# Squared-ReLU attention with a routed feed-forward on one core: order of the work at the end of a slot and of a chunk, and the share of squares on ScalarE

## The chip, the core and the metric

One core of a Trainium2 chip. TensorE (PE in the profile, PEld for its weight loads) multiplies, VectorE is DVE, ScalarE is ACT, GpSimd is POOL, SyncE (SP) issues nearly all transfers. The metric is device time in microseconds of one execution, lower is better; the kernel before has a median of 2253.57 us over 3 runs.

## What is computed

```python
scores = (1/S) * z @ z.T                    # z: (8, 3136, 64)
attn   = np.maximum(scores, 0.0) ** 2
x      = u * (attn @ v)                     # u, v: (8, 3136, 256), S = 3136
# then, for each batch: the 128 rows of x with the largest x @ w_gate go through
xe + sigmoid(score) * (np.maximum(xe @ w1, 0) @ w2)      # w1: (256, 1024), w2: (1024, 256)
```

All in float32. Since z @ z.T is symmetric, a square of one block serves, turned, as the square of the mirrored block.

## The kernel before

The eight batches follow one another. A batch has seven chunks of output columns, five of 512, one of 256 and one of 320 (`chunks_of`), and a chunk has thirteen slots: twelve take two 128-row blocks of the summed dimension each, the thirteenth the 64 rows left over. The text numbers chunks 0 to 6 and slots 0 to 12.

A slot that is new computes its scores (`scores`, L478): six matmuls into one pair of banks `sc` (L510), a ReLU into `a` (L514, ACT), then squares. The square is kept as two parts for the matmuls, `hi` (L524, ACT, rounded) and `lo`, the exact square less `hi` (L614, on POOL or DVE). So the exact square `a` is needed too: either on ACT (L530) or on DVE (L534), as the rule at L529 says from a running estimate of each engine's backlog (`busy`). New squares that a later chunk needs are turned on DVE (L577, L595, L557) and stored to DRAM; a slot that is old reads them back (`qk`) and makes `hi` by a copy (L474). Scores run three slots ahead (`LEAD`).

`mix` (L649) writes the PE work of one slot: twelve steps of two matmuls (L641), which use the upper and the lower 64 rows at once and add to four banks `acc`. A phase is the half of the steps that goes to one pair of these banks. An ordinary slot runs eight steps with `hi`, then `between` (the scores of the slot three ahead), then four with `lo`. Slot 0 runs phase 0, `between`, phase 1. Slot 11, the ending one, runs its phase 0 (`one`), then the phase 0 of slot 12 (the 64 rows, `Vr`), which closes two banks, then its phase 1 (`two`). The small matmuls of routing and feed-forward (`beside`) stand in front of step 4.

There are five `acc` banks in turn, so a new chunk has one free bank and takes the others from the old chunk: its phase 0 needs the first bank that ACT copied out (`finish_early`, L720, two copies into `x`), its phase 1 the other copied bank and the one that the first DVE instruction of `finish` releases (L732). `finish` (L724) adds the other two banks to `x` (L732), multiplies by u (L736), and after that turns and stores the result (L745, L752).

Instructions of an engine run in the order in which this program writes them. What follows a `mix` on DVE and ACT (the `posts` of the small matmuls and the squares, turns and `lo` of the slot three ahead) is written behind it.

Of the kernel before, what the change touches and what calls it, by code (L numbers as in the profile page):

```python
# [15 lines left out]
ALU = mybir.AluOpType  # L16
# [72 lines left out]
def attention_then_routed_ffn(ctx: ExitStack, tc: tile.TileContext, zt, ut, v, wg, w1, w2, cst, cst16, keys, outs, at, cap):  # L89
# [388 lines left out]
    def scores(k):  # L478
        b, c, js, is_old = slots[k]
        if is_old:  # L480
            return old_scores(k)
        n = len(js)
        w = CHUNKS[c][1]
        mov = Z[b, c]
        hi = work.tile([P, 2, CH], F32R, name="hi", tag="hi2", bufs=LEAD)
        a = work.tile([P, 2, CH], F32, name="a", tag="a", bufs=3)
        ps = ps_s.tile([P, 2, CH], F32, name="sc", tag="sc")
        if n == 1:
            w = w // 2
            o = js[0] * P - WIDE  # L490
            for i, (z, m) in enumerate(((ZHe, 0), (ZHe, 1), (ZLe, 0))):
                for q in range(2):
                    rows = slice(q * 64, q * 64 + 64)
                    nc.tensor.matmul(  # L494
                        ps[:, q, :w], z[rows, o : o + P], mov[m][rows, q * w : (q + 1) * w], start=i == 0, stop=i == 2
                    )
            a, hi = a[:, 0, :w], hi[:, :, within(c)]
            for q in range(2):
                rows = slice(q * 64, q * 64 + 64)
                nc.scalar.activation(a[rows], ps[rows, q, :w], AF.Relu)  # L500
            nc.scalar.activation(hi[:, 0, :w], a, AF.Square)
            spend(act=0.39 + 0.0024 * w)
            lows.append((k, a, hi[:, :, :w], (), lambda: nc.vector.tensor_tensor(a, a, a, op=ALU.mult)))
            return
        if is_second(k):
            mov, w = [x.rearrange("p (f x) -> p f x", x=P)[:, :, P // 2 :] for x in mov], w // 2
        for i, (high, m) in enumerate(((True, 0), (True, 1), (False, 0))):
            for q in range(2):
                rows = slice(q * 64, q * 64 + 64)
                nc.tensor.matmul(  # L510
                    ps[:, q, :w], stationary(high, js[0] // 2, q), mov[m][rows], start=i == 0, stop=i == 2
                )
        a = a[:, :, :w]
        nc.scalar.activation(a, ps[:, :, :w], AF.Relu)  # L514
        act = 0.13 + 0.0016 * w
        spend(act=act)
        if is_second(k):
            by = lambda x: x.rearrange("p q (f x) -> p q f x", x=P)
            pieces = [(lambda x: by(x)[..., 64:], a.rearrange("p q (f x) -> p q f x", x=64))]
            pieces.append((lambda x: by(x)[..., :64], fetched[b, c, c].rearrange("p f (q x) -> p q f x", q=2)))  # L520
        else:
            hi = hi[:, :, within(c)]
            pieces = [(lambda x: x, a)]
        nc.scalar.activation(pieces[0][0](hi), pieces[0][1], AF.Square)  # L524
        for view, src in pieces[1:]:
            nc.scalar.copy(view(hi), src)
        spend(act=act * len(pieces))
        dve = 0.15 + 0.00208 * w
        if busy["act"] + act < busy["dve"] + dve + (0.16 + 0.00236 * w if turns(k) else 0.0):  # L529
            nc.scalar.activation(a, a, AF.Square)  # L530
            spend(act=act)
            square = lambda: None
        else:
            square = lambda: nc.vector.tensor_tensor(a, a, a, op=ALU.mult)  # L534
            spend(dve=dve)
        lows.append((k, a, hi, pieces, square))

    def turns(k):
        b, c, js, _ = slots[k]
        return (c < WHOLE or c == WHOLE and b < B - 1) and js[0] * P >= sum(CHUNKS[c])  # L540
# [108 lines left out]
    def mix(k, beside, between):  # L649


        b, c, js, _ = slots[k]
        assert k in parts
        first, last = k % SLOTS == 0, js[0] == NJ
        ending = k % SLOTS == SLOTS - 2
        if first:
            banks = [ps_a.tile([P, CH], F32, name="acc", tag="acc")[:, : CHUNKS[c][1]] for _ in range(2 * NK)]
            acc[b, c] = [[banks[0], banks[2]], [banks[3], banks[1]]]
        if last:
            todo = steps_of(k, 1)  # L660
            turn = 3
        else:
            one, two = (steps_of(k, phase) for phase in range(2))
            if ending:
                todo, turn = [*one, *steps_of(k + 1, 0), lambda: finish_early(b, c), *two], 6
            elif first:
                todo, turn = [*one, *two], 6
            else:
                todo, turn = [*one[:4], *two[:4], *one[4:], *two[4:]], 8
        for n, step in enumerate(todo):  # L670
            if n == min(4, turn):
                for op in beside:
                    op()
            if n == turn:
                between()
            step()
        parts.pop(k)
        if turn == len(todo):
            if last:
                near.extend(finish(b, c))  # L680
            between()
# [42 lines left out]
    def finish(b, c):  # L724

        scored = c < NCH - merged(b)
        c0, w = CHUNKS[c]
        NB = w // Q
        xT = chunk.pop((b, c))
        whole, sums = early.pop((b, c))  # L730
        for h in reversed(range(NK)):
            nc.vector.scalar_tensor_tensor(  # L732
                sums[h], acc[b, c][1 - h][h], SCALE * SCALE, sums[h], op0=ALU.mult, op1=ALU.add
            )
        for h in range(NK):
            nc.vector.tensor_tensor(xT[:, h, :w], sums[h], xT[:, h, :w], op=ALU.mult)  # L736
        spend(dve=0.2 + 0.0046 * w)
        del acc[b, c]
        if c == 0:
            gate[b] = tail.tile([P, TP], F32, name="gate", tag="gate")  # L740
        x = whole[:, :NB]
        wx = xT.rearrange("p h c -> p (h c)").rearrange("p (f r) -> p f r", r=RUN)[:, :NB]

        def turn(h):
            nc.vector.transpose(x[:, :, h, :], xT[:, h, :w].rearrange("p (f q) -> p f q", q=Q))  # L745
            spend(dve=0.1 + 0.0013 * w)
            if h < NK - 1:
                return
            to = outs[b][c0 : c0 + w, :].rearrange("(f t) (g r) -> g t f r", t=Q, g=NG)
            runs = x.rearrange("p f h r -> p f (h r)")  # L750
            for g in range(NG):
                stores.append(lambda g=g: nc.sync.dma_start(to[g], runs[g * Q : (g + 1) * Q]))  # L752
            if scored:
                nc.gpsimd.tensor_tensor(  # L754
                    wx,
                    runs,
                    consts["wg_run"].rearrange("p (o r) -> p o r", o=1).broadcast_to([P, NB, RUN]),
                    op=ALU.mult,
                )
                spend(pool=0.1 + 0.0042 * w)  # L760

        def add():
            nc.vector.tensor_reduce(gate[b][:, c0 // Q : c0 // Q + NB], wx, axis=AX.X, op=ALU.add)
            spend(dve=0.1 + 0.0023 * w)

        def flip(i):

            h, i = i % NK, i // NK
            o, n = groups_of(w)[i]
            if h == 0:  # L770
                flipped.append(ps_a.tile([P, 512], F32, name="flip", tag="acc"))
            nc.tensor.transpose(flipped[i][:n, h * P : (h + 1) * P], xT[:, h, o : o + n], consts["ident"])

        def store(i):
            o, n = groups_of(w)[i]
            to = whole.rearrange("p f h r -> p (f h r)")[:n, i * D : (i + 1) * D]
            src = flipped[i][:n, :D].rearrange("p (h g r) -> p g h r", h=NK, g=NG)
            nc.scalar.copy(to.rearrange("p (g h r) -> p g h r", g=NG, h=NK), src)
            stores.append(lambda: nc.sync.dma_start(outs[b][c0 + o : c0 + o + n, :], to))

        flipped = []
        turns = [lambda h=h: turn(h) for h in range(NK)]
        if scored:
            return [([], turns), ([], [None, add])]
        spread, seen = scores_of(b, c, xT)
        if c == NCH - 1:
            flips = [([lambda i=i, h=h: flip(i * NK + h) for h in range(NK)], lambda i=i: store(i)) for i in range(-(-w // P))]
            return [(spread, None), ([], [lambda q=q: seen(q) for q in range(2)]), *flips]
        return [(spread, turns), ([], [lambda q=q: seen(q) for q in range(2)])]
# [949 lines left out]
```

## Time and profile before

| | before |
|---|---|
| runs | 2240.06, 2253.57, 2254.3 us (median 2253.57) |
| the profiled execution | 2252.5 us, span of its instructions 2250.7 us |
| mean granted TensorE clock | 0.978 of full speed |
| busy share PE / DVE / ACT / POOL | 92% / 79% / 60% / 64% |
| matmuls | 19700, of them 16800 of L641 |

Times within a row are microseconds, unless ns stands there. In rows of waits an arrow points to the engine and line that ended the wait. In rows of the timeline the first number is the start from the span's beginning, the second the time from the start of the first to the end of the last of the instructions that the row merges (xN), and brackets hold the idle time of the engine before it.

### The profile page before, as it was taken

The page shows a single profiled execution, that of the slowest core. Times are in us where ns is not written, and L with a number is a line of the kernel's source. Part 1 is how long each engine was busy: PE and PEld are TensorE (multiplying, and loading weights), DVE is VectorE, ACT ScalarE, POOL GpSimd, SP SyncE. Part 2 cuts the span into 40 slices and gives each one's busy share as a digit, 9 for nine tenths or more (in the row PEclk, how much of TensorE's full clock was granted, in tenths as well). Part 3 has the DMA queues.
Part 4 walks back from the last instruction along what each step waited for, and adds up shares of the span by engine and source line. Part 5 has one row for each costly group of instructions (what it writes and reads, how often), then busy time and mean ns, then how long its engine had stood idle before and what let it go on. Part 6 is the DMA issues. An engine that isn't in the chain of part 4 may idle for free.

```text
span 2250.7 us, 51225 instructions
## 1 busy us (share of the span) xinstructions
PE 2081.2 (92%) x19700; PEld 1743.9 (77%) x19700; DVE 1772.1 (79%) x2771; ACT 1360.9 (60%) x1846; POOL 1438.8 (64%) x773
## 2 busy tenths in 40 slices
PE   7899989999898999989999999999999999889897
PEld 5688978779776797778877788777887789667686
DVE  8887799757997589976889668986698887867665
ACT  6565667556774476745676556664576656666452
POOL 5776587646875467855678457765578665766452
PEclk9999999999999999999999999999999999999998
DMA  5678757785577865777567776667756687546841
GB/s 168 190 214 233 209 164 226 213 224 171 173 206 197 222 180 167 210 208 218 175 186 192 206 217 191 181 185 193 229 175 198 161 206 214 168 132 165 210 141 70
DMA packets 450869, 426.94 MB, mean 190 GB/s; under 512 B 136576, under 2 KB 377792, under 8 KB 447808
## 3 DMA queue, kind: packets, MB, share of 16 engines
q1 hardware_dynamic: 449488, 421.18, 66.0%
q8 instruction: 154, 2.52, 0.5%
q0 software_dynamic: 768, 2.10, 0.3%
q14 instruction: 91, 0.75, 0.1%
q10 hardware_dynamic: 368, 0.39, 0.1%
HBM read 248.94 MB, written 174.60 MB: 188 GB/s over the span
## 4 chain that ended last, share of the span: by engine, by line
PE 39%; DVE 23%; DMA 15%; issue 8%; SPq 6%; ACT 5%; POOL 3%; DVEq 0%; ACTq 0%; POOLq 0%
PE acc L641 33%; DVE aT L577 5%; DMA qk<-squares 5%; DVE a L534 4%; PE sc L510 3%; DMA squares<-aT 3%; DVE lo L614 3%; DVE ut L736 3%; POOL lo L614 2%; ACT hi L524 2%; DMA qk<-squares_narrow 1%; ACT a L514 1%; DMA squares_narrow<-aT 1%; SPq L752 1%; DMA zst<-in_zt 1%
## 5 line engine op out<-in xcount | busy, mean ns | idle before, releaser
L641 PE MATMUL acc<-hi,V 64*128 64x512 f32 (+2 forms) x10752 | 1320.5, 367 | 31.0 <-ACT x L720 20.5
L641 PEld LDWEIGHTS acc<-hi,V 64*128 64x128 f32 x10752 | 1008.7, 188 | 209.7 <-ACT x L720 39.7
L614 POOL TENSOR_TENSOR lo<-a,hi 128x1024 fp32r<-128x1024 f32 (+1 forms) x320 | 721.2, 2255 | 554.2 <-DVE a L534 336.1
L641 PE MATMUL acc<-lo,V 64*128 64x512 f32 (+2 forms) x5376 | 742.2, 369 | 57.0 <-POOL lo L614 43.7
L641 PEld LDWEIGHTS acc<-lo,V 64*128 64x128 f32 x5376 | 523.5, 188 | 145.7 <-POOL lo L614 67.6
L514 ACT ACTIVATE a<-sc 128x1024 f32<-128x1024 f32 (+2 forms) x345 | 327.5, 949 | 378.8 <-PE sc L510 329.8
L474 ACT CAST hi<-qk 128x1024 fp32r<-128x1024 f32 (+2 forms) x327 | 279.9, 858 | 257.6 <-PE acc L641 195.8
L534 DVE TENSOR_TENSOR a<-a 128x1024 f32<-128x1024 f32 (+1 forms) x203 | 288.6, 1422 | 146.5 <-ACT hi L524 144.6
L524 ACT ACTIVATE hi<-a 128x1024 fp32r<-128x1024 f32 (+2 forms) x345 | 339.7, 985 | 35.4 <-PE acc L641 8.7
L614 DVE TENSOR_TENSOR lo<-qk,hi 128x1024 fp32r<-128x1024 f32 (+2 forms) x213 | 299.4, 1417 | 77.9 <-ACT hi L474 70.4
L577 DVE STREAM_TRANSPOSE aT<-a 128x512 f32<-128x512 f32 (+1 forms) x494 | 317.2, 680 | 50.8 <-DMA squares<-aT 30.4
L614 POOL TENSOR_TENSOR lo<-qk,hi 128x1024 fp32r<-128x1024 f32 (+2 forms) x114 | 230.0, 2023 | 97.4 <-issue 51.3
L736 DVE TENSOR_TENSOR ut<-x,ut 128x512 f32<-128x512 f32 (+2 forms) x112 | 184.8, 1689 | 1.9
L754 POOL TENSOR_TENSOR ut<-x,w_run 128x1024 f32<-128x1024 f32 (+2 forms) x52 | 130.2, 2503 | 77.6 <-DVE x L745 69.2
L126 POOL TENSOR_TENSOR V<-vst,V 128x512 fp32r<-128x512 f32 x92 | 168.6, 1844 | 15.4 <-ACT V L125 13.3
L530 ACT ACTIVATE a<-a 128x1024 f32<-128x1024 f32 (+2 forms) x142 | 144.1, 1015 | 4.5
L510 PE MATMUL sc<-Z,ZH 64*128 64x512 f32 x480 | 107.5, 380 | 5.3 <-ACT a L514 5.2
L732 DVE SCALAR_TENSOR_TENSOR x<-acc,x 128x512 f32<-128x512 f32 (+2 forms) x112 | 64.4, 616 | 54.4 <-ACT x L720 48.8
L510 PE MATMUL sc<-Z,ZL 64*128 64x512 f32 x480 | 105.2, 371 | 0.0
L510 PE MATMUL sc<-Zl,ZH 64*128 64x512 f32 x480 | 104.7, 371 | 0.0
L500 ACT ACTIVATE a<-sc 64x256 f32<-64x256 f32 (+2 forms) x112 | 39.4, 351 | 91.8 <-PE sc L494 86.8
L126 POOL TENSOR_TENSOR ZL<-zst,ZH 64x256 fp32r<-64x256 f32 x70 | 69.6, 995 | 13.3 <-ACT ZH L125 10.7
(219 smaller groups left out, 1867.0 us busy)
## 6 DMA issues: line engine op xcount, KB each, us to landing
squares<-aT SPq DMA_DIRECT2D x160, 512.0 KB, 3.3
qk<-squares SPq DMA_DIRECT2D x320, 256.0 KB, 6.2
squares_narrow<-aT SPq DMA_DIRECT2D x320, 128.0 KB, 3.8
qk<-squares_narrow SPq DMA_DIRECT2D x80, 512.0 KB, 4.4
out<-x SPq DMA_DIRECT2D x162, 128.0 KB, 3.5
ut<-in_ut SPq DMA_DIRECT2D x40, 512.0 KB, 5.6
vst<-in_v SPq DMA_DIRECT2D x158, 128.0 KB, 3.4
zmv<-in_zt SPq DMA_DIRECT2D x78, 128.0 KB, 4.1
```

What stands on the lines that cost most here:

```text
L126: (lo_on or nc.vector.tensor_tensor)(lo, src, hi.bitcast(F32), op=ALU.subtract)
L474: nc.scalar.copy(by(hi), src)
L510: nc.tensor.matmul(ps[:, q, :w], stationary(high, js[0] // 2, q), mov[m][rows], start=i == 0, stop=i == 2)
L514: nc.scalar.activation(a, ps[:, :, :w], AF.Relu)
L524: nc.scalar.activation(pieces[0][0](hi), pieces[0][1], AF.Square)
L530: nc.scalar.activation(a, a, AF.Square)
L534: square = lambda: nc.vector.tensor_tensor(a, a, a, op=ALU.mult)
L577: nc.vector.transpose(to, a[:, q].rearrange("p (m t a) -> p m t a", m=GT, a=Q))
L614: on.tensor_tensor(view(lo), src, view(hi).bitcast(F32), op=ALU.subtract)
L641: nc.tensor.matmul(bank[g][h][:, cols[g]], V[b, j][rows, i, h], mov[rows], start=(b, c, g, h) not in opened, stop=len(js) == 1 and n == 2,)
L736: nc.vector.tensor_tensor(xT[:, h, :w], sums[h], xT[:, h, :w], op=ALU.mult)
L754: nc.gpsimd.tensor_tensor(wx, runs, consts["wg_run"].rearrange("p (o r) -> p o r", o=1).broadcast_to([P, NB, RUN]), op=ALU.mult,)
```

## The change

Four edits. The test at L529 lets a square go to ScalarE as long as its backlog is less than DVE's plus 1.0 and the cost on DVE (before: ScalarE's backlog with this square added had to be less than DVE's with its own cost). `mix` writes `beside` behind the last step of a slot, where it stood in front of step 4. In the ending slot `between` moves from behind `one` to behind the early steps of slot 12, and `finish_early` stands in front of it. `finish` adds within the PSUM bank (`rest`) and multiplies from there, bank by bank, where it added into `x` for both banks first.

```diff
@@ scores
-        if busy["act"] + act < busy["dve"] + dve + (0.16 + 0.00236 * w if turns(k) else 0.0):
+        if busy["act"] < busy["dve"] + 1.0 + dve + (0.16 + 0.00236 * w if turns(k) else 0.0):
             nc.scalar.activation(a, a, AF.Square)
@@ mix
             if ending:
-                todo, turn = [*one, *steps_of(k + 1, 0), lambda: finish_early(b, c), *two], 6
+                early_steps = steps_of(k + 1, 0)
+                todo, turn = [*one, *early_steps, *two], len(one) + len(early_steps)
...
         for n, step in enumerate(todo):
-            if n == min(4, turn):
-                for op in beside:
-                    op()
             if n == turn:
+                if ending:
+                    finish_early(b, c)
                 between()
             step()
+        for op in beside:
+            op()
@@ finish
         for h in reversed(range(NK)):
-            nc.vector.scalar_tensor_tensor(
-                sums[h], acc[b, c][1 - h][h], SCALE * SCALE, sums[h], op0=ALU.mult, op1=ALU.add
-            )
-        for h in range(NK):
-            nc.vector.tensor_tensor(xT[:, h, :w], sums[h], xT[:, h, :w], op=ALU.mult)
+            rest = acc[b, c][1 - h][h]
+            nc.vector.scalar_tensor_tensor(rest, rest, SCALE * SCALE, sums[h], op0=ALU.mult, op1=ALU.add)
+            nc.vector.tensor_tensor(xT[:, h, :w], rest, xT[:, h, :w], op=ALU.mult)
```

New line numbers: L722 is L720 of before, L735 is L732, L736 stays.

Over the program 119 of 203 squares of L534 leave DVE for ACT (L530: 142 before, 261 after). Since the backlog estimates shift, 55 of the `lo` subtractions also leave POOL for DVE.

First place, PE, slot 9 of chunk 2 (of batches 1 to 5): `ahead` is a routing count, two small matmuls that read `upto` of DVE. Before:

```order
L641 MATMUL acc<-hi,V 128x512 x8
L1038 LDWEIGHTS c_86
L1038 MATMUL ahead<-upto,c_86 98x2
L1039 LDWEIGHTS c_86
L1039 MATMUL ahead<-upto,c_86 98x2
L641 MATMUL acc<-hi,V 128x512 x8
L494 MATMUL sc<-Z,ZHe 128x256 x2
L494 MATMUL sc<-Zl,ZHe 128x256 x2
L494 MATMUL sc<-Z,ZLe 128x256 x2
L641 MATMUL acc<-lo,V 128x512 x8
```

Now:

```order
L641 MATMUL acc<-hi,V 128x512 x16
L494 MATMUL sc<-Z,ZHe 128x256 x2
L494 MATMUL sc<-Zl,ZHe 128x256 x2
L494 MATMUL sc<-Z,ZLe 128x256 x2
L641 MATMUL acc<-lo,V 128x512 x8
L1038 LDWEIGHTS c_86
L1038 MATMUL ahead<-upto,c_86 98x2
L1039 LDWEIGHTS c_86
L1039 MATMUL ahead<-upto,c_86 98x2
```

The pair moved past eight matmuls with `hi`, the scores and eight with `lo`, to the end of its slot.

Second place, the end of chunk 2. On ACT, before:

```order
L474 CAST hi<-qk 128x1024
L514 ACTIVATE a<-sc 128x1024
L524 ACTIVATE hi<-a 128x1024
L720 ACTIVATE x<-acc 128x512 x2
L474 CAST hi<-qk 128x1024
```

Now:

```order
L474 CAST hi<-qk 128x1024
L722 ACTIVATE x<-acc 128x512 x2
L514 ACTIVATE a<-sc 128x1024
L524 ACTIVATE hi<-a 128x1024
L474 CAST hi<-qk 128x1024
```

The two copies out of `acc` moved ahead of the ReLU and the square of the next chunk's slot 1. On DVE at the same place, before:

```order
L614 TENSOR_TENSOR lo<-qk,hi 128x1024
L534 TENSOR_TENSOR a<-a 128x1024
L732 SCALAR_TENSOR_TENSOR x<-acc,x 128x512 x2
L736 TENSOR_TENSOR ut<-x,ut 128x512 x2
L595 STREAM_TRANSPOSE aT<-a 128x8x32 x2
```

Now:

```order
L614 TENSOR_TENSOR lo<-qk,hi 128x1024
L534 TENSOR_TENSOR a<-a 128x1024
L735 SCALAR_TENSOR_TENSOR acc<-acc,x 128x512
L736 TENSOR_TENSOR ut<-acc,ut 128x512
L735 SCALAR_TENSOR_TENSOR acc<-acc,x 128x512
L736 TENSOR_TENSOR ut<-acc,ut 128x512
L595 STREAM_TRANSPOSE aT<-a 128x8x32 x2
```

Sum and product now alternate; the exact square of the next chunk's slot 1 still stands in front of them on DVE (at the ends of chunks 2 and 3 of every batch).

Third place, DVE at the end of chunk 0, where slots 0 and 1 of the next chunk are both new. Before:

```order
L557 STREAM_TRANSPOSE aT<-a 128x256
L534 TENSOR_TENSOR a<-a 128x1024
L595 STREAM_TRANSPOSE aT<-a 128x8x32 x2
L534 TENSOR_TENSOR a<-a 128x1024
L732 SCALAR_TENSOR_TENSOR x<-acc,x 128x512 x2
L736 TENSOR_TENSOR ut<-x,ut 128x512 x2
L951 TENSOR_SCALAR ge,own<-gates,k_sb 128x392
```

Now:

```order
L557 STREAM_TRANSPOSE aT<-a 128x256
L595 STREAM_TRANSPOSE aT<-a 128x8x32 x2
L614 TENSOR_TENSOR lo<-a,hi 128x1024
L735 SCALAR_TENSOR_TENSOR acc<-acc,x 128x512
L736 TENSOR_TENSOR ut<-acc,ut 128x512
L735 SCALAR_TENSOR_TENSOR acc<-acc,x 128x512
L736 TENSOR_TENSOR ut<-acc,ut 128x512
L951 TENSOR_SCALAR ge,own<-gates,k_sb 128x392
```

Both squares left for ACT, and the `lo` of the next chunk's slot 0, which was POOL's, stands on DVE behind the turns L595.

## Rows read from the trace of the kernel before

**Rows 1.** The page: span, and busy time and share of each engine.

```profile
span 2250.7 us, 51225 instructions
...
PE 2081.2 (92%) x19700; PEld 1743.9 (77%) x19700; DVE 1772.1 (79%) x2771; ACT 1360.9 (60%) x1846; POOL 1438.8 (64%) x773
```

**Rows 2.** Waits of PE: for whom, us in total, times, longest.

```profile
PE acc L641 <- POOL lo L614: 43.7, 44, 3.3
PE ahead L1038 <- DVE upto L1031: 20.5, 7, 3.7
PE acc L641 <- ACT x L720: 20.5, 32, 1.8
PE tot L903 <- DVE cnt L897: 15.6, 9, 4.8
...
PE h L1358 <- DVE xs L126: 8.6, 5, 2.8
...
PE gate L862 <- DVE gate L763: 6.5, 4, 1.8
```

**Rows 3.** Timeline, batch 3: chunk 2, slot 9, then an undisturbed slot of chunk 4.

```profile
958.97 0.16 PE L1038 MATMUL ahead<-upto,c 98*98 98x2 bf16 x1 [3.69 <-DVE upto L1031]
...
1048.63 1.98 PE L641 MATMUL acc<-hi,V 64*128 64x512 f32 x16
...
1050.44 0.28 PE L494 MATMUL sc<-Z,ZHe 64*128 64x256 f32 x2
...
1050.80 1.09 PE L641 MATMUL acc<-lo,V 64*128 64x512 f32 x8
```

**Rows 4.** Timeline, batch 4: end of chunk 2 and start of chunk 3.

```profile
1241.76 0.40 PE L510 MATMUL sc<-Z,ZH 64*128 64x512 f32 x2
...
1242.45 0.52 PE L641 MATMUL acc<-hi,Vr 64*128 64x256 f32 x6
...
1244.03 1.06 ACT L524 ACTIVATE hi<-a 128x1024 fp32r<-128x1024 f32 x1 [0.34 <-PE acc L641]
...
1244.99 1.06 ACT L720 ACTIVATE x<-acc 128x512 f32<-128x512 f32 x2
1245.12 1.23 DVE L534 TENSOR_TENSOR a<-a 128x1024 f32<-128x1024 f32 x1 [3.44 <-ACT hi L524]
...
1245.62 1.19 PE L641 MATMUL acc<-hi,V 64*128 64x512 f32 x7 [0.68 <-ACT x L720]
...
1246.26 1.28 DVE L732 SCALAR_TENSOR_TENSOR x<-acc,x 128x512 f32<-128x512 f32 x2
...
1247.58 4.62 DVE L736 TENSOR_TENSOR ut<-x,ut 128x512 f32<-128x512 f32 x2
1247.58 1.29 PE L641 MATMUL acc<-hi,V 64*128 64x512 f32 x8
```

**Rows 5.** Timeline, batch 3: start of chunk 1, DVE.

```profile
881.15 0.77 DVE L595 STREAM_TRANSPOSE aT<-a 128x256 f32<-128x256 f32 x2 [2.51 <-DMA squares_narrow<-aT]
```

**Rows 6.** Timeline, batch 3: chunk 0, slots 2 and 3, PE.

```profile
841.75 1.21 PE L641 MATMUL acc<-lo,V 64*128 64x512 f32 x8 [1.34 <-POOL lo L614]
...
847.41 0.88 PE L641 MATMUL acc<-lo,V 64*128 64x512 f32 x4 [1.93 <-DVE lo L614]
```

**Rows 7.** Groups of DVE by line and shape: busy us, mean ns, idle before.

```profile
L534 DVE TENSOR_TENSOR a<-a 128x1024 f32<-128x1024 f32 x156 | 246.7, 1582 | 141.1 <-ACT hi L524 139.6
...
L736 DVE TENSOR_TENSOR ut<-x,ut 128x512 f32<-128x512 f32 x80 | 152.8, 1948 | 1.4
...
L732 DVE SCALAR_TENSOR_TENSOR x<-acc,x 128x512 f32<-128x512 f32 x80 | 51.4, 684 | 40.7 <-ACT x L720 36.9 <-DMA vst<-in_v 3.8
...
L1393 DVE TENSOR_TENSOR hl<-hT,hh 128x512 fp32r<-128x512 f32 x16 | 10.8, 687 | 12.2 <-ACT hh L1389 12.2
```

**Rows 8.** Stretches of time, PE: length, busy (instructions), granted clock, DMA share, GB/s.

```profile
958.00:962.00 4.00, 3.03 (x24) 0.81 0.44 136
962.00:966.00 4.00, 4.00 (x30) 0.76 0.88 218
...
941.00:945.00 4.00, 4.00 (x39) 1.00 0.87 272
```

## The prediction

> **What bounds the kernel now.** I read the page first: PE is busy 92% of a span of 2250.7 us, DVE 79%, POOL 64%, ACT 60% [rows 1]. PE is the bound, so an edit is worth what it takes out of PE's idle time, about 170 us, and of the time at a lower clock. Next I read whom PE waits for [rows 2]. Three kinds matter here: for POOL's `lo` (43.7 us), for the copies out of `acc` at a chunk's start (20.5 us), and for DVE in front of a small matmul (`ahead`, `tot`, `h`, `gate`: 20.5 + 15.6 + 8.6 + 6.5 = 51.2 us). Then I read the timeline at these places [rows 3 to 6], the durations on DVE by shape [rows 7], and the granted clock behind a long wait [rows 8].
>
> **The change, part by part.**
>
> *Small matmuls at the slot's end.* In slot 9 of chunk 2 PE stands 3.69 us, with matmuls of the slot ready behind, until DVE has `upto` [rows 3]. Now eight matmuls with `hi`, the scores and eight with `lo` come first. Sixteen take 1050.44 - 1048.63 = 1.81 us, so eight take 0.9; scores of half width take 0.36 (1050.80 - 1050.44) [rows 3], of full width 0.69 (1242.45 - 1241.76) [rows 4]. I take eight `lo` at the same 0.9. The shift is thus 2.2 us, or 2.5. The seven `ahead` waits keep 20.5 - 7 x 2.2 = 5.1 us. Of nine `tot` waits the longest, 4.8, keeps 2.3; the others have a mean of 1.35 and vanish. Of `h` 0.3 stays, of `gate` nothing. 7.7 of 51.2 us stay: **-43.5 us**. Bounds: 0, if DVE's result comes later by as much, and -51.2. What waits now instead are the instructions on DVE and ACT that read these matmuls, 2 us later than before, with `lo` of the slot three ahead queued behind them; PE needs that two slots later (a slot without scores is 24 matmuls, 2.7 us), which covers it. Without the cover it would cost the same 2 us back.
>
> *Copies ahead of the squares.* At the start of chunk 3 PE idles 0.68 us for the first copy, which starts at 1244.99 because the square at 1244.03 stood in front of it [rows 4]. Now the copies start when the small group of slot 12 is done. That group takes about 0.36 us (as scores of that width), so its last matmul ends near 1242.3, the copies run to 1243.4, and PE finds its bank. What is late next is the second half of slot 0, which needs the first bank that DVE releases. The chain there: ReLU to 1244.5 (taken as long as the square), square to 1245.6, where it ended at 1245.09 before, exact square on DVE 1.23 us to 1246.8, sum 0.64, product 0.69, release at 1248.2. Before, the sum alone released it, at 1246.26 + 0.64 = 1246.9, and PE came at 1247.58. PE would now come at 1247.58 - 0.68 = 1246.9, waits 1.3 us and goes on 0.6 later than before. At the start of chunk 4 the order on DVE is the same and no scores (0.69) stand between PE's halves, so there it is 1.3 later. Eight batches: **+15 us**. Where DVE has neither exact square nor `lo` in front (starts of chunks 5 and 6) a part of the wait of 20.5 us is won: **-2 us**.
>
> *DVE in front of the sum at chunk 1.* The turns L595 sat until 881.15 for a transfer that read their buffer, and took 0.77 us [rows 5]. `lo`, which POOL did, now stands behind them on DVE: 881.9 + 1.2 = 883.1, at best. Phase 0 of slot 0 needs it about 0.9 us after the slot begins, near 881.4. That is up to 1.8 us of wait in place of 0.68 plus a lost pair of matmuls (0.23), or 0.9 worse at eight starts, +7; nothing if the buffer comes free earlier. **+4 us**.
>
> *Finish within the bank.* The product from SBUF and SBUF takes 1948 ns, the sum with one operand in PSUM 684, and L1393, a difference with one operand in PSUM and this shape, 687 [rows 7]. I take 684 for the new sum (its output in PSUM is not in the trace; bounds 0 saved, and 1948) and 687 for the product. 80 products of this shape save 1.26 us each, 101 us of DVE. DVE idles 21%, so I count this at nothing; its effect is in the next item.
>
> The Trainium skill (VectorE: DVE Perf Modes, Rules for kernel authors) speaks against this edit: it advises a copy from PSUM to SBUF first where many operations follow on a matmul's output. By the page's fixed costs, 120 against 58 cycles at 0.96 GHz, a PSUM operation is 65 ns dearer, an estimate of 15 us of DVE over 224 operations and 7 us on the path (two per chunk start), and the sum of this text would be 2203. The trace shows the opposite here, 687 against 1948 ns.
>
> *More squares on ScalarE, and chunk 0.* 119 squares leave DVE, at up to 1582 ns [rows 7], and cost ACT about 1.06 us each (as the square at 1244.03 [rows 4]), 126 us at most on an engine that idles 40%: that cover makes them free. Without it, where ReLU queues behind the added square, PE waits for `sc`. The edit pays in chunk 0, where each slot is new: PE waits 1.34 us for `lo` in slot 2 and 1.93 in slot 3 [rows 6]. Both follow on the 4.62 us of the two products [rows 4], now 1.4, and on squares that DVE no longer does; slot 3's `lo` also leaves DVE. Seven batches, 22.9 us. At the start of chunk 0 one added square (1.06 us) stands in front of a ReLU for which the next scores wait: 7 x 1.06 = 7.4 back. **-15 us**; bounds +7 and -23.
>
> *POOL.* 55 `lo` leave it. Of its 43.7 us [rows 2] 9.4 are in slot 2 above (seven times 1.34); of the other 34 I take a seventh: **-5 us**; bounds 0 and -34.
>
> *Clock.* Behind the wait at 958.97 the granted clock was 0.81 and 0.76 over two stretches of 4 us, between the two levels 1.2 and 2.4 GHz, against 1.00 at 941 [rows 8]: 4 x (0.19 + 0.24) = 1.7 us lost. Seven such waits fall to a size below 1.5 us: 12 us, less some for the new waits: **-10 us**. Bounds: 0, and -49 (the mean clock of 0.978 over the span).
>
> Sum: -43.5 + 15 - 2 + 4 - 15 - 5 - 10 = -56.5. From the profiled execution's 2252.5 us this gives **2196 us** (it lies 1 us under the median of the runs, 2253.57).
>
> **The rivals.** *All of it is won.* DVE is early enough at each chunk start, so the 20.5 us are won instead of paid for, and half of what the clock costs comes back: -51.2 - 20.5 - 22.9 - 25 = -120, 2133 us. For it: 101 us less of products on DVE. Against: the idle time of 139.6 us in front of L534 [rows 7] says that DVE waits there for ACT, not for its own work, and that chain is not shorter.
>
> *The small matmuls win nothing.* Their inputs are made on DVE, which follows PE's pace; if DVE's queue holds them back as much as before, -43.5 and the clock's -10 are gone: 2250 us, no change. For it: DVE is in order, and new waits at chunk starts push it back. Against: PE runs 2.2 us of its own work in that time, which DVE need not wait for.
>
> *Slower.* DVE's `lo` in front of the sum at the ends of chunks 0, 1 and 6, some 23 starts, runs while POOL works. The two products of 4.62 us, 0.69 each with a PSUM operand, show that such an overlap adds 1.6 us to an operation [rows 4, 7]. Added to the release of the bank and to phase 0, and with a drop of the clock of 1.7 us each, this is 23 x 3.3 = 76 us: 2272 us. It outweighs the rest from 56 us on, that is from 2.4 us per such start.
>
> **How the numbers follow.** Forecast 0.55 (2160 to 2230), all won 0.18 (2110 to 2160), small matmuls win nothing 0.17 (2220 to 2250), slower 0.10 (2255 to 2300). A measurement of this kernel can tell about 1% from no change, 22 us. Faster by more than that, under 2230: nearly all of the first two and a part of the third, 0.74; within it 0.16; slower 0.10. The range 2130 to 2250 leaves out the slower case and the lower part of the second.
>
> **What would show it.** Right: the waits of `ahead`, `tot`, `h` and `gate` fall to under 10 us; that of PE on the copies is gone and PE waits for the product L736 instead, some 1 to 2.5 us at the starts of chunks 3 and 4; the product takes 0.7 us; ACT is busy near 1490 us and DVE under 1650; chunk 0's waits in slots 2 and 3 are gone. Wrong: PE's wait for L736 sums to over 60 us, PE's wait of `sc` for ACT grows past 20, or the four small-matmul waits stay above 30.

## The result

The changed kernel took 2129.36 us (median of 4 runs, 2125.69 to 2133.84) against 2253.94 before: a ratio of 0.9464, 95% interval 0.9426 to 0.9501. The direction was forecast and most of the places too, but the size was not: 125 us were won where 56 were forecast, and the time lies 0.6 us under the range.

The page after, as in [rows 1]: the span, and busy time and share of each engine.

```profile
span 2132.1 us, 51160 instructions
...
PE 2037.6 (96%) x19700; PEld 1756.1 (82%) x19700; DVE 1536.0 (72%) x2707; ACT 1462.7 (69%) x1965; POOL 1315.4 (62%) x718
```

PE's idle time fell from 169.5 to 94.5 us. The mean granted clock rose from 0.978 to 0.985: what it fell short of full speed was 0.022 x 2250.7 = 49.5 us and is now 0.015 x 2132.1 = 32.0.

The waits of PE after, as in [rows 2]: for whom, us in total, times, longest.

```profile
PE acc L641 <- DVE lo L614: 26.0, 7, 4.7
PE acc L641 <- DVE ut L736: 20.6, 21, 3.4
PE acc L641 <- POOL lo L614: 14.1, 22, 2.4
PE sc L510 <- ACT a L514: 9.5, 10, 1.1
...
PE tot L903 <- DVE cnt L897: 2.4, 1, 2.4
```

The waits for the copies (20.5), `ahead` (20.5) and `h` (8.6) are gone, that for POOL is a third of what it was. Two have taken their place: 20.6 us for the product, L736, and 26.0 for a `lo` that DVE makes, 25.7 of them at the start of chunk 1. A `lo` of DVE was waited for before too, but in slot 3 of chunk 0 (before):

```profile
PE acc L641 <- DVE lo L614: 11.7, 6, 2.0
```

DVE after, by line and shape, as in [rows 7]: busy us, mean ns, idle before.

```profile
L736 DVE TENSOR_TENSOR ut<-acc,ut 128x512 f32<-128x512 f32 x80 | 55.3, 692 | 2.7
L735 DVE SCALAR_TENSOR_TENSOR acc<-acc,x 128x512 f32<-128x512 f32 x80 | 55.3, 691 | 23.7 <-PE acc L641 23.6
```

The product takes 692 ns for 1948, and the sum written to PSUM 691 for 684: both durations came out as taken.

`ahead`, in a timeline of PE after (batch 1, chunk 2, slot 9; start, length), to be read against [rows 3]:

```profile
396.14 1.10 PE L641 MATMUL acc<-lo,V 64*128 64x512 f32 x8
397.17 0.21 PE L1038 MATMUL ahead<-upto,c 98*98 98x2 bf16 x1
397.24 0.18 PE L1039 MATMUL ahead<-upto,c 98*98 98x2 bf16 x1
397.35 1.88 PE L641 MATMUL acc<-hi,V 64*128 64x512 f32 x14
```

No wait stands in brackets, and the granted clock is 1.00 in each stretch of 4 us from 390 to 402. The start of chunk 1 is the place that got worse (after, batch 4; all engines):

```profile
1094.86 1.06 ACT L530 ACTIVATE a<-a 128x1024 f32<-128x1024 f32 x1
...
1099.96 0.77 DVE L595 STREAM_TRANSPOSE aT<-a 128x256 f32<-128x256 f32 x2 [4.92 <-DMA squares_narrow<-aT]
1100.12 2.35 POOL L614 TENSOR_TENSOR lo<-a,hi 128x1024 fp32r<-128x1024 f32 x1 [5.71 <-DMA squares_narrow<-aT]
1100.66 2.89 DVE L614 TENSOR_TENSOR lo<-a,hi 128x1024 fp32r<-128x1024 f32 x1
1102.42 3.35 POOL L614 TENSOR_TENSOR lo<-qk,hi 128x1024 fp32r<-128x1024 f32 x1
...
1103.60 1.15 PE L641 MATMUL acc<-lo,V 64*128 64x512 f32 x4 [4.68 <-DVE lo L614]
```

Slot 0's square was ready at 1094.86 + 1.06 = 1095.92. Its `lo`, now on DVE, stood behind turns that waited 4.92 us for a transfer, and then ran beside POOL's `lo` of another slot: it ended 1.1 us after POOL's did (1100.12 + 2.35 = 1102.47), 2.89 us after its start. PE waited 4.68 us for it. Then the granted clock was 0.59 over 4 us, near the lower of its two levels (after; length, busy, granted clock, DMA share, GB/s):

```profile
1103.00:1107.00 4.00, 3.40 (x16) 0.59 0.25 82
1107.00:1111.00 4.00, 4.00 (x36) 0.98 0.22 77
```

### The profile page after: what moved, and what is told of

The parts are those of the page before. It is cut to its first block, busy times and chain, and to the rows that moved or that the text cites. A ratio compares the mean times of both kernels' runs of the same rounds, so it can differ in the third digit from the quotient of the medians.

```text
span 2132.1 us, 51160 instructions
## 1 busy us (share of the span) xinstructions
PE 2037.6 (96%) x19700; PEld 1756.1 (82%) x19700; DVE 1536.0 (72%) x2707; ACT 1462.7 (69%) x1965; POOL 1315.4 (62%) x718
## 4 chain that ended last, share of the span: by engine, by line
PE 68%; DMA 7%; DVE 5%; ACT 4%; SPq 3%; issue 2%; POOL 1%; POOLq 0%; ACTq 0%; DVEq 0%
PE acc L641 58%; PE sc L510 7%; DMA qk<-squares 2%; DMA zst<-in_zt 2%; ACT a L514 1%; ACT hi L524 1%; DVE lo L614 1%; PE h L1358 1%; DMA squares_narrow<-aT 1%; DMA squares<-aT 1%; DVE a L534 1%; DVE aT L577 1%; PE y L1401 1%; DVE acc L735 1%; SPq L589 1%
## 5 line engine op out<-in xcount | busy, mean ns | idle before, releaser
L641 PE MATMUL acc<-hi,V 64*128 64x512 f32 (+2 forms) x10752 | 1270.5, 364 | 22.9 <-DVE ut L736 20.6
L641 PEld LDWEIGHTS acc<-hi,V 64*128 64x128 f32 x10752 | 1004.3, 186 | 158.6 <-issue 30.2
L614 POOL TENSOR_TENSOR lo<-a,hi 128x1024 fp32r<-128x1024 f32 (+1 forms) x280 | 634.2, 2267 | 462.0 <-ACT a L530 207.5
L641 PE MATMUL acc<-lo,V 64*128 64x512 f32 (+2 forms) x5376 | 716.4, 364 | 40.4 <-DVE lo L614 26.0
L641 PEld LDWEIGHTS acc<-lo,V 64*128 64x128 f32 x5376 | 520.1, 186 | 106.8 <-DVE lo L614 29.4
L614 POOL TENSOR_TENSOR lo<-qk,hi 128x1024 fp32r<-128x1024 f32 (+2 forms) x112 | 220.8, 1979 | 137.9 <-ACT hi L474 122.1
L530 ACT ACTIVATE a<-a 128x1024 f32<-128x1024 f32 (+2 forms) x261 | 256.4, 982 | 7.5
L534 DVE TENSOR_TENSOR a<-a 128x1024 f32<-128x1024 f32 (+1 forms) x84 | 153.4, 1827 | 63.2 <-ACT hi L524 56.3
L126 POOL TENSOR_TENSOR V<-vst,V 128x512 fp32r<-128x512 f32 x92 | 161.5, 1764 | 17.8 <-ACT V L125 17.2
L754 POOL TENSOR_TENSOR ut<-x,w_run 128x1024 f32<-128x1024 f32 (+2 forms) x52 | 131.5, 2529 | 37.1 <-DVE x L745 36.8
L614 DVE TENSOR_TENSOR lo<-a,hi 128x1024 fp32r<-128x1024 f32 (+2 forms) x65 | 83.8, 1289 | 24.4 <-ACT a L530 22.0
L735 DVE SCALAR_TENSOR_TENSOR acc<-acc,x 128x512 f32<-128x512 f32 (+2 forms) x112 | 70.0, 625 | 26.4 <-PE acc L641 26.2
L722 ACT ACTIVATE x<-acc 128x512 f32<-128x512 f32 (+2 forms) x112 | 54.5, 538 | 45.4 <-PE acc L641 44.5
```

The source lines that it names most:

```text
L126: (lo_on or nc.vector.tensor_tensor)(lo, src, hi.bitcast(F32), op=ALU.subtract)
L614: on.tensor_tensor(view(lo), src, view(hi).bitcast(F32), op=ALU.subtract)
L641: nc.tensor.matmul(bank[g][h][:, cols[g]], V[b, j][rows, i, h], mov[rows], start=(b, c, g, h) not in opened, stop=len(js) == 1 and n == 2,)
L735: nc.vector.scalar_tensor_tensor(rest, rest, SCALE * SCALE, sums[h], op0=ALU.mult, op1=ALU.add)
L754: nc.gpsimd.tensor_tensor(wx, runs, consts["wg_run"].rearrange("p (o r) -> p o r", o=1).broadcast_to([P, NB, RUN]), op=ALU.mult,)
```

## The experiments

All times below are medians over three rounds (4 to 10 runs) beside runs of the kernel before (2249 to 2251 us), with the ratio to it and its interval. I also read each trace by place: the time from a slot's first matmul L641 to the next slot's, summed over the eight batches, less the same in the kernel before. The four edits alone, with the short diffs:

```diff
 beside: mix
-            if n == min(4, turn):
-                for op in beside:
-                    op()
...
             step()
+        for op in beside:
+            op()
 finish: finish
...
-                sums[h], acc[b, c][1 - h][h], SCALE * SCALE, sums[h], op0=ALU.mult, op1=ALU.add
...
-            nc.vector.tensor_tensor(xT[:, h, :w], sums[h], xT[:, h, :w], op=ALU.mult)
+            rest = acc[b, c][1 - h][h]
+            nc.vector.scalar_tensor_tensor(rest, rest, SCALE * SCALE, sums[h], op0=ALU.mult, op1=ALU.add)
+            nc.vector.tensor_tensor(xT[:, h, :w], rest, xT[:, h, :w], op=ALU.mult)
 squares: scores
-        if busy["act"] + act < busy["dve"] + dve + (0.16 + 0.00236 * w if turns(k) else 0.0):
+        if busy["act"] < busy["dve"] + 1.0 + dve + (0.16 + 0.00236 * w if turns(k) else 0.0):
 copies: mix, the ending slot
-                todo, turn = [*one, *steps_of(k + 1, 0), lambda: finish_early(b, c), *two], 6
+                early_steps = steps_of(k + 1, 0)
+                todo, turn = [*one, *early_steps, *two], len(one) + len(early_steps)
...
+                if ending:
+                    finish_early(b, c)
```

**The small matmuls alone.**

> The kernel before with one edit: the small matmuls stand behind the last step of their slot. Theory PLACE (each place is won by the edit that touches it): the waits on ahead, tot, h and gate vanish with the lower clock behind them; by the time per slot, before against after, that is 28 us in slot 9 of chunk 2, 16 in slot 9 of chunk 3 and some 12 elsewhere, so 55 us less, about 2198. Theory ROOM (the products and squares that left DVE make it early, and that wins most of the waits): DVE is as late as before, its results come late at the slot's end too, at most 20 us less, about 2233, and ahead plus tot still wait over 20 us.

Measured: 2195.06, ratio 0.976 (0.973 to 0.979). 

**The finish alone.**

> The kernel before with one edit: sum and product within the PSUM bank. PLACE: DVE works 100 us less, PE gains nothing by it, and the first bank comes free 0.7 us later at each of 48 chunk starts, some of which wait: 0 to 10 us more, about 2257. ROOM: PE's waits for lo in slots 2 and 3 of chunk 0 and in slot 6 of chunk 1 go (27 and 19 us) and a third of those of the small matmuls (20 us): 60 us less, about 2193.

Measured: 2189.57, ratio 0.9747 (0.9719 to 0.9775). 

**The squares alone.**

> The kernel before with one edit: the rule that gives more squares to ScalarE (and with it 55 of the lo to DVE). PLACE: chunk 0's slots 2 and 3 (29 us) and slot 6 of chunk 1 (21 us) are won here, and the start of chunk 1 pays 25 us for lo behind the turns on DVE: 25 us less, about 2228. ROOM: the products of 4.6 us still hold DVE at each chunk start, so no more than 10 us less, about 2244; chunk 1's start pays in either case.

Measured: 2200.81, ratio 0.9774 (0.9742 to 0.9805). 

**The copies alone.**

> The kernel before with one edit: the copies out of acc and the early steps ahead of the next scores. Both theories: PE's wait of 20 us for the copies goes, and about half comes back as a wait for the first sum of DVE, since the scores and with them the squares in front of that sum come later: 10 us less, about 2243. What would differ from both: over 30 us less (the start of a chunk cost more than its waits show) or any more time than before.

Measured: 2241.16, ratio 0.9963 (0.9948 to 0.9977).

So 54, 60, 48 and 8 us. PLACE holds for the small matmuls and ROOM for the finish; the squares win twice the larger of the two expectations, which neither theory explains: a large part is in slot 9 of chunk 2, named by neither. Together they are 170 us, and the whole change wins 125: several edits remove the same waits. By place (us, each column against the kernel before):

| place | whole | small matmuls | finish | squares | copies |
|---|---|---|---|---|---|
| chunk 0, slot 2 | -11.5 | -0.1 | -11.8 | -11.5 | 0.7 |
| chunk 0, slots 3, 4 | -25.1 | -0.4 | -6.1 | -25.0 | -1.9 |
| chunk 1, slot 0 | 30.0 | 0.1 | 3.4 | 34.6 | -5.0 |
| chunk 1, slot 6 | -21.0 | -3.1 | -18.7 | -19.4 | -1.1 |
| chunk 2, slot 9 | -28.3 | -20.4 | -8.7 | -22.8 | -7.4 |
| chunk 3, slots 8, 9 | -22.5 | -7.2 | -24.0 | -9.7 | 4.1 |
| slot 0 of chunks 2 to 6 | 0.9 | -6.8 | 17.0 | 29.3 | -10.9 |
| all other slots | -40.3 | -20.7 | -17.0 | -20.3 | 7.0 |

But for the program's two ends the columns add up to the differences of the profiled executions (118.6, 59.2, 66.3, 46.3 and 15.2 us of span), up to 7 us away from those of the medians: the execution that was profiled for the copies was the fastest of its ten.

How the finish wins is to be seen in chunk 1 (before, batch 3; DVE, POOL and PE in a timeline, brackets are idle time and what ended it):

```profile
884.26 4.62 DVE L736 TENSOR_TENSOR ut<-x,ut 128x512 f32<-128x512 f32 x2
...
900.58 0.67 DVE L745 STREAM_TRANSPOSE x<-ut 128x512 f32<-128x512 f32 x1
...
901.33 2.40 POOL L754 TENSOR_TENSOR ut<-x,w_run 128x1024 f32<-128x1024 f32 x1 [3.80 <-DVE x L745]
903.68 4.74 POOL L614 TENSOR_TENSOR lo<-a,hi 128x1024 fp32r<-128x1024 f32 x2
...
906.10 1.21 PE L641 MATMUL acc<-lo,V 64*128 64x512 f32 x8 [1.90 <-POOL lo L614]
```

From the product to the second turn of the result, L745, DVE works without idle time, 17 us long. POOL waits 3.80 us for that turn, its two `lo` stand behind, and PE waits for the first. With the finish alone (batch 3, the same place; L743 and L752 are L745 and L754):

```profile
875.54 0.67 DVE L743 STREAM_TRANSPOSE x<-ut 128x512 f32<-128x512 f32 x1
...
876.29 2.40 POOL L752 TENSOR_TENSOR ut<-x,w_run 128x1024 f32<-128x1024 f32 x1 [0.24 <-DVE x L743]
878.64 4.78 POOL L614 TENSOR_TENSOR lo<-a,hi 128x1024 fp32r<-128x1024 f32 x2
```

POOL waits 0.24, and PE waits no more in that slot. The squares' rule frees the same queue by other means, so each wins these 19 us alone, and together they win 21.

What the squares pay without the copies' edit shows in their run's waits of PE:

```profile
PE acc L641 <- ACT x L720: 55.5, 46, 2.0
```

At the starts of chunks 1, 3 and 4 one square more (1.06 us) stands on ACT in front of the copies, and PE waits about 1.77 us there, where it waited 0.68 in the kernel before.

**The whole change without one edit each** (the edits above, undone one at a time in the changed kernel).

> The changed kernel without the finish within the bank (sums into SBUF first, then products from SBUF). Alone, the four edits won 60 (finish), 54 (beside), 48 (squares) and 8 us (copies), 170 together, while the whole change won 120. Theory SAME PLACES (several edits remove the same waits: slot 2 of chunk 0 and slot 6 of chunk 1 go with the finish or with the squares, slot 9 of chunks 2 and 3 with any of three): the other three edits still remove them, and the first bank comes free 0.7 us earlier, so 0 to 10 us from the changed kernel, 2125 to 2140. Theory SHARES (each edit gives about 0.7 of what it gave alone, by a DVE that is less loaded everywhere): 42 us lost, 2171.

Measured: 2139.45, ratio 0.9503 (0.9474 to 0.9532).

> The changed kernel without the new rule for squares (and so without the lo that moved to DVE). SAME PLACES: slot 3 of chunk 0 (17 us), slot 4 (4) and slot 11 of chunk 5 (6) come back, since no other edit removed them, and the 30 us that the start of chunk 1 pays go: about 2130, no change within 8 us. SHARES: 34 us lost, 2163.

Measured: 2142.56, ratio 0.951 (0.9485 to 0.9535).

> The changed kernel with the small matmuls back in front of step 4. SAME PLACES: squares and finish together still remove most of the waits in slot 9 of chunks 2 and 3; tot and gate come back with the lower clock behind them, 15 to 20 us: about 2147. SHARES: 38 us lost, 2167.

Measured: 2175.47, ratio 0.9654 (0.9628 to 0.9681).

> The changed kernel with the copies and the early steps in their old order. SAME PLACES: with more squares on ScalarE the copies stand behind one more of them at chunk starts, as the run with the squares alone showed (PE waited 55.5 us for copies there, 20.5 before), so this edit is worth 35 to 45 us here though 8 alone: about 2168. SHARES: 6 us lost, 2135.

Measured: 2159.46, ratio 0.9586 (0.9561 to 0.9612).

Beside the 0.9464 of the whole, the finish is worth 0.4% there, the squares 0.5%, the copies 1.2% and the small matmuls 1.9%. The first two are not told apart from nothing: the intervals overlap that of the whole. SAME PLACES comes nearest for the first three, though the squares (2143 for 2130, with 8 us either way) and the copies (2159 for 2168) lie outside its figures. What is worth 60 alone is worth about 10 at most when others remove the same waits, and what is worth 8 alone is worth about 30, because the squares make it needed: without it PE waits 45.2 us for the copies. For the small matmuls 2175 is above both expectations. PE's waits in that run:

```profile
PE acc L641 <- DVE ut L737: 31.5, 29, 3.0
...
PE tot L904 <- DVE cnt L898: 15.9, 10, 5.5
...
PE ahead L1039 <- DVE upto L1032: 5.8, 7, 1.8
PE h L1359 <- DVE xs L126: 4.7, 4, 1.8
```

`tot`, `ahead`, `h` and `gate` (2.1) sum to 28.5, which the other edits do not remove, where I had put 15 to 20. The other 10.9 us are in the wait for the product, 8.2 of them at the start of chunk 4: there it is 1.87 us in each of batches 1 to 5, and nothing in the changed kernel (this run, batch 4):

```profile
1245.10 1.16 PE L641 MATMUL acc<-hi,V 64*128 64x512 f32 x7 [1.87 <-DVE ut L737]
```

The reason is in the changed kernel's end of chunk 3 (after, batch 4):

```profile
1225.40 0.73 PE L1358 MATMUL h<-wh,xs 128*128 128x512 f32 x2
...
1226.62 1.22 DVE L534 TENSOR_TENSOR a<-a 128x1024 f32<-128x1024 f32 x1 [3.48 <-ACT hi L524]
...
1226.99 0.62 PE L641 MATMUL acc<-hi,Vr 64*128 64x256 f32 x6
...
1227.76 0.69 DVE L735 SCALAR_TENSOR_TENSOR acc<-acc,x 128x512 f32<-128x512 f32 x1
```

Behind the last step of slot 11 now stands `h`, 1.6 us of PE's work between the two halves of the chunk's end, and in that time DVE makes the square that stands in front of the sum. Only batches 1 to 5 have `h` there; in batches 0, 6 and 7 the changed kernel does wait, 3.39, 2.00 and 1.89 us. At the end of chunk 2 only a short `taken` stands there, and PE waits (after, batch 4):

```profile
1184.46 1.23 DVE L534 TENSOR_TENSOR a<-a 128x1024 f32<-128x1024 f32 x1 [2.25 <-ACT hi L524]
...
1187.16 1.16 PE L641 MATMUL acc<-hi,V 64*128 64x512 f32 x7 [0.87 <-DVE ut L736]
```

Without the finish, the waits that come back in chunk 3 (slots 8 and 9, 19 us) are for ACT (waits of PE in that run):

```profile
PE sc L494 <- ACT a L514: 8.9, 5, 2.9
PE acc L641 <- ACT hi L526: 8.5, 5, 2.0
PE acc L641 <- DVE x L734: 6.8, 6, 2.6
```

ACT is late because a transfer is, and the transfer because of DVE (batch 3 of that run; the first row, a wait of SyncE from 920 to 948, then the timeline):

```profile
SPq L597 <- DVE aT L595: 8.9, 1, 8.9
...
944.69 1.05 ACT L474 CAST hi<-qk 128x1024 fp32r<-128x1024 f32 x1 [4.16 <-DMA qk<-squares]
...
952.05 0.62 ACT L526 CAST hi<-vst 128x512 fp32r<-128x512 f32 x1 [2.93 <-DMA vst<-squares_own]
...
952.72 2.10 PE L641 MATMUL acc<-hi,V 64*128 64x512 f32 x16 [2.01 <-ACT hi L526]
```

The turns L595 stand behind the products on DVE, SyncE waits for them with the store of their result, 8.9 us where it is 4.7 in the changed kernel, and the transfers that SyncE issues behind it come later. The store goes out 8.4 us after the chunk's first matmul, 5.2 in the changed kernel; ACT's wait for `qk` is 0.18 there.

**The finish, with its saved time filled again.** In the kernel with the finish alone:

```diff
         x = whole[:, :NB]
+        for h in (0, 1, 0, 1):
+            nc.vector.transpose(x[:, :, h, :], xT[:, h, :w].rearrange("p (f q) -> p f q", q=Q))
```

> The kernel before with the finish within the bank alone (2189.57 us in its run), and behind its two products four turns on DVE more (two of them done twice), 4 x 0.68 = 2.7 us in a chunk of 512, about the 2.5 us that the faster products save there. Theory TIME (the edit wins because DVE's queue behind the finish is 2.5 us earlier): the gain is nearly gone, 2235 to 2250; slot 6 of chunk 1 waits for lo again. Theory CONTENTION (a product with both operands in SBUF and POOL's lo slow each other, so it is POOL that is earlier): the turns have one operand in SBUF and slow nothing, the gain stays, 2185 to 2205.

Measured: 2251.29, ratio 1.0004 (0.9984 to 1.0023). The gain is gone, so TIME: DVE is busy 1763.2 us in this run, 1662.5 with the finish alone and 1772.1 before. PE's wait for POOL in this run:

```profile
PE acc L641 <- POOL lo L614: 24.0, 29, 2.8
```

One part of that expectation failed: slot 6 of chunk 1 gave back 5 of 18.7 us, and POOL's `lo` waits stay at 24.0 (22.1 with the finish alone, 43.7 before). The trace shows that the four turns did not make DVE as late there as it had been (this run, batch 3):

```profile
893.93 2.40 POOL L754 TENSOR_TENSOR ut<-x,w_run 128x1024 f32<-128x1024 f32 x1 [1.91 <-PE acc L641]
```

From the first product to the end of the second turn of the result DVE takes 16.0 us, 14.4 with the finish alone and 17.0 before; POOL's L754 starts 2.3 us before the slot's first matmul, for 4.0 and 0.2. So slot 6 does not speak against TIME. The loss lies elsewhere: 12 us in slots 8 and 9 of chunk 3, 6 in slot 9 of chunk 2, 7 in slots 2 to 4 of chunk 0, 27 spread over other slots. Of the 58 us between the two traces 34 are idle time of PE (129.6 to 163.8) and 21 the clock (0.991 to 0.982). So the total is a matter of DVE's time.

**Where the moved `lo` belong.** Two changes of the changed kernel: all choices of an engine for `lo` as before, by a list; and only slot 0 of chunk 1 kept on POOL.

```diff
 lo_as_before
-                if busy["pool"] + took > busy["dve"] + dve + (1.2 if busy["pool"] > 0 else 0.0):
+                if next(LO_BEFORE) == "D":
 pin_lo
-                if busy["pool"] + took > busy["dve"] + dve + (1.2 if busy["pool"] > 0 else 0.0):
+                if busy["pool"] + took > busy["dve"] + dve + (1.2 if busy["pool"] > 0 else 0.0) and not (c == 1 and k % SLOTS == 0):
```

> The changed kernel, with every lo on the engine (POOL or DVE) that it had before; the squares stay as changed. Theory SQUARES (the squares on ScalarE win, the moved lo only costs): the start of chunk 1 falls by 27 us, slot 3 of chunk 0 stays good since DVE no longer has its squares, 2103 to 2110. Theory LO (the moved lo is a part of the gain): slot 3 of chunk 0 (its lo went from DVE to POOL in six batches) gives back 15 us, POOL has 55 lo more and waits of 15 to 25 us for it come back, so 2125 to 2140.

Measured: 2107.24, ratio 0.9365 (0.9336 to 0.9394).

> The changed kernel, with the lo of slot 0 in chunk 1 kept on POOL (it had moved to DVE in six batches, behind turns that wait for a transfer, and then ran 2.9 us beside POOL). The wait on DVE lo of 4.9 us at six chunk starts goes, POOL stands idle there from 1094.5 to 1100.1 in batch 4 and can take it: 26 us less, 2103. If instead the wait belongs to the turns (the sum of DVE stands behind them too), PE meets a wait for the sum 1 to 2 us later and no more than 15 us are won, 2115.

Measured: 2114.34, ratio 0.9389 (0.9359 to 0.9418). Its largest wait of PE:

```profile
PE acc L641 <- DVE ut L736: 31.4, 29, 3.1
```

SQUARES holds: the side effect of the new rule, the `lo` that move, costs 22 us. Chunk 0's slots 3 and 4 keep 22 of their 25 us, so the squares that left DVE won them. In the second run the start of chunk 1 falls by 23 us, and the wait for the product rises by 10.8: behind the turns, which still wait for their transfer, now stand sum and product. That is the case of 15 us that the expectation named.

**The first bank released earlier**, with that `lo` on POOL:

```diff
             rest = acc[b, c][1 - h][h]
-            nc.vector.scalar_tensor_tensor(rest, rest, SCALE * SCALE, sums[h], op0=ALU.mult, op1=ALU.add)
-            nc.vector.tensor_tensor(xT[:, h, :w], rest, xT[:, h, :w], op=ALU.mult)
+            into = sums[h] if h else rest
+            nc.vector.scalar_tensor_tensor(into, rest, SCALE * SCALE, sums[h], op0=ALU.mult, op1=ALU.add)
+        for h, total in enumerate((acc[b, c][1][0], sums[1])):
+            nc.vector.tensor_tensor(xT[:, h, :w], total, xT[:, h, :w], op=ALU.mult)
```

> As the run before, and the sum of the first bank goes to SBUF, so that this bank is free after the sum (0.7 us earlier), while the second bank keeps its sum and product; the product of the first, from SBUF and SBUF, comes last. If PE's waits for L736 at chunk starts (20.6 us) are the release alone, up to 0.7 us at each of 21 starts is won, 12 us, 2091. If the slow product (1.95 us for 0.69) pushes back what stands behind it on DVE, as the kernel without the finish showed in chunk 3 (slots 8 and 9, 19 us), it loses as much as it wins: 2100 to 2110.

Measured: 2098.92, ratio 0.9315 (0.9283 to 0.9347), the best of all. Its waits of PE:

```profile
PE acc L641 <- DVE x L736: 10.5, 11, 2.3
...
PE sc L494 <- ACT a L514: 7.0, 5, 2.2
```

The product from SBUF and SBUF in this kernel, among the groups of DVE (busy us, mean ns, idle before):

```profile
L738 DVE TENSOR_TENSOR ut<-x,ut 128x512 f32<-128x512 f32 x40 | 47.7, 1193 | 0.0
```

The wait at chunk starts falls from 31.4 to 10.5, and 6 us come back in slots 8 and 9 of chunk 3: between the two expectations, and a gain of 15 us over the run before.

## Why the prediction was right or wrong

**The small matmuls (-43.5, and most of the clock's -10): right.** The four waits went from 51.2 to 2.4 us, where 7.7 were left standing. The edit alone left 8.6 of them (`tot` 5.1, `ahead` 3.5) and won 54, so the rival by which it wins nothing is out. In the whole change it is worth less than alone, since the other edits make the same results earlier.

**The copies (+15 at the starts of chunks 3 and 4, -2 at others): right in kind, too large.** The wait moved from the copies to the product, as forecast, and at chunk 3 it is 0.87 us in the row above where 1.3 was worked out. But slot 0 of chunks 2 to 6 together cost 0.9 us instead of 13. A step that failed: "At the start of chunk 4 the order on DVE is the same". On PE it is not. I moved the small matmuls to the slot's end in one item and forgot them in the next, where they stand in the gap that I was pricing. Without them there the price was right: in the run that puts them back, slot 0 of chunks 3 and 4 takes 0.52 and 1.18 us longer than in the kernel before (batch 1), where 0.6 and 1.3 were worked out.

**The start of chunk 1 (+4): wrong, 30.** I priced DVE's `lo` at 1.2 us behind the turns; it took 2.89, beside POOL's. And the turns themselves came later: their transfer let them begin 2.14 us after the slot's first matmul (1099.96 - 1097.82), where 881.15 [rows 5] is 0.86 after it (880.29); why was not followed. The first part is the mechanism of my rival *slower* (DVE's `lo` beside POOL's), at six starts instead of 23. The run that kept this `lo` on POOL shows the 23 us at that slot.

**The finish: the step that failed.** "DVE idles 21%, so I count this at nothing; its effect is in the next item." The edit alone wins 60 us, as much as any, and the run that fills the saved time again wins nothing. The mean of 21% hid stretches such as the 17 us in chunk 1 in which DVE's queue does not pause and POOL and PE stand at its end. I had counted only chunk 0 for it. In the whole change the squares relieve the same queue, and the finish's own share there is not told apart from nothing. What the sum lacked is the relief of DVE's queue, whichever of the two gives it: slot 6 of chunk 1 (-21.0, with POOL's 5 us forecast for all places), and slot 9 of chunk 2 with slots 8 and 9 of chunk 3 (-50.8, where the small matmuls alone win 27.6).

**Squares and chunk 0 (-15): too small.** Slots 2 and 3 gave 29.0 us, not 22.9, and slot 4, which was not priced, 7.6. The products in front of chunk 0 are not those of 4.62 us, as I had it, but those of the chunk of 320 columns, 3.58 us for the two (before, 833.24). The 7.4 taken off for a late ReLU came about: in slot 0 of chunk 0 PE waits 7.2 us for it over the eight batches, 0.8 before (after, batch 4):

```profile
1055.49 0.50 PE L510 MATMUL sc<-Z,ZH 64*128 64x512 f32 x2 [0.95 <-ACT a L514]
```

In the whole program that wait only went from 5.2 to 9.5, since others of its kind vanished. ACT is busy 1462.7 us (1490 forecast) and that cover held, but not in front of the copies: without their edit the squares cost 35 us more there. I had put this under neither edit.

**POOL (-5): wrong, by the same step as the finish.** A seventh of 34 us was a guess about 55 `lo` that left POOL. What moved was slot 6 of chunk 1 (-21) and slot 11 of chunk 5 (-6), and in slot 6 POOL was late because it waited for DVE.

**The clock (-10):** 17.5 us by the means of the two pages.

The two profiled executions are 118.6 us apart by their spans, 62 more than forecast, and 26 us more loss at chunk 1 than forecast hide a part of what was missed: the lateness that reached PE and POOL through DVE's queue. The rival *all won* named 2133, but not for its reasons: the chunk starts were not won, so that its number came close is luck. Of the signs for being right all came but the size of the wait for L736; they watched the places that had been priced.

The prediction set 687 against 1948 ns to say that an operand in PSUM is the faster one. The comparison holds only beside POOL's work (before, batch 7; POOL is idle while the two products run):

```profile
2163.38 1.29 DVE L736 TENSOR_TENSOR ut<-x,ut 128x512 f32<-128x512 f32 x2
...
2165.41 1.33 POOL L614 TENSOR_TENSOR lo<-qk,hi 128x512 fp32r<-128x512 f32 x1 [3.02 <-ACT hi L474]
```

These two took 691 and 683 ns from SBUF and SBUF, as long as from PSUM (692). The Trainium skill (VectorE: DVE Perf Modes, Rules for kernel authors) leaves the choice between taking the operand from PSUM and copying it to SBUF first where many operations follow. Here PSUM was the better choice, because nearly all of these products run beside POOL.

## What to carry to other kernels

Read an engine's share of busy time by stretches, not over the span: an operation on an engine that idles a fifth of the time can still hold a queue at whose end others wait. Where several edits aim at the same waits, undo each in the whole as well as trying it alone: here the sum of the parts was 170 us, the whole 125, and the edit worth least alone was worth 30 in company. Look for what a changed estimate moves besides its target: 55 `lo` that nobody meant to move cost 22 us. And before a duration is put down to where an operand lies, look for the same instruction without its neighbours' work: 683 ns and 1948 on average were one and the same product.

## What the runs showed of the hardware

An operation of DVE with two SBUF operands and one of POOL that overlap slow each other more than I had priced: at the start of chunk 1 `lo` on DVE took 2.89 us and ended 1.1 us after POOL's had ended, and POOL's next, which began beside it at 1102.42, took 3.35 where the one before took 2.35.

The Trainium skill (SBUF — State Buffer, Who interferes with whom) says that a DVE instruction with two inputs in SBUF and a GpSimd instruction that reads SBUF contend for a shared port, that this port is an exclusive lock, and that the order of issue decides which of them blocks. These rows agree: DVE's 2.89 us are the 1.81 until POOL's end and 1.08 of its own, and POOL's 3.35 are the 1.13 until DVE's end and 2.22 of its own.

The products show it too, 128x512 each. From SBUF and SBUF they took 677 to 691 ns in the 4 of 80 that met no instruction of POOL (before), and 2015 on average in the other 76. In the whole without the finish it is 679 to 692 ns in 9 and 1851 in 71. In the best kernel, where 40 products have this form, the average is still 1193. With one operand in PSUM all 80 of the changed kernel took 691 to 693 ns, though 78 of them met POOL. No run took POOL's work away; the comparison is between instances of one instruction in the same kernels.
